# Fewer VectorE instructions in weight preparation and in the aside exponential, and row copies by transfer instead of ScalarE, in a two-layer attention and gated-MLP kernel

## The chip, the cores and the metric

The kernel runs on one core of a Trainium2 chip. The metric is the device time of one execution in microseconds (us); lower is better. The engines are named as the profile names them: PE (TensorE), PEld (its weight loads), DVE (VectorE), ACT (ScalarE), POOL (GpSimd, called Pool below) and SP (SyncE, which here only issues transfers).

## The reference

Two identical layers on x of 2048 tokens by 448 features, in float32. The same weights serve both layers.

```python
def _A_ref(x, wqkv, wo):                       # 16 heads of 28
    qkv = (x @ wqkv).reshape(B, S, 3, H, Dh).transpose(2, 0, 3, 1, 4)
    q, k, v = qkv[0], qkv[1], qkv[2]
    p = softmax(einsum("bhqd,bhkd->bhqk", q, k) * Dh ** -0.5)
    return einsum("bhqk,bhkd->bhqd", p, v).transpose(0, 2, 1, 3).reshape(B, S, D) @ wo
def _B_ref(x, w_gate, w_up, w_down):           # F = 1792
    return (sigmoid(x @ w_gate) * (x @ w_up)) @ w_down
x = x + _A_ref(layernorm(x), wqkv, wo)
x = x + _B_ref(layernorm(x), w_gate, w_up, w_down)
# ... the same two lines once more
```

## The kernel before, in words

**Numbers in two parts.** PE multiplies float16 tiles. A float32 operand is held as a high part (its float16 rounding) and a low part (what that left out), and a product is high by high, low by high and high by low.

**Half tiles.** The q/k projection and the gate and up products use Strassen's scheme with sums of quarter blocks. A block of 512 tokens is prepared by `Block.half_steps`: 10 or 11 small steps named after the quarters and differences (`r11, t1, t2, t3, r21, t4, r22, [r12], last_low, last_rows`), which leave the tiles `wide` (four operands) and `short` (three or four); ACT makes the high parts (`high`), DVE the differences and low parts (`subtract`, `low`). Of the 448 features the last 64 half-fill a tile, so the upper 64 partitions of some slots are free; `again` (L486) copies 64 rows of high parts into such a slot with ACT, and `last_rows` (L547, L548) adds and copies 64 more rows. A block is "turned" when its features come by PE transposes (the first block of each gated stage, two in all); the other blocks read them back through memory. Twelve blocks are made in all.

The weights for these products are made once, in layer 0, by `split_sums`: for a pair of weight tiles it forms four sums (`add_up`, L263), 14 high half tiles (L269) and their low parts (L272) in one float16 tile `t` of 27 slots (`N_SUMS`), with Pool copying some 64-partition halves (L290, L291) and DVE adding one pair (L292). The tile is written to memory (`gu_parts`, `qs_parts`, L1409) and loaded where it is used. `of_halves` (L656) multiplies; `LOW_A`, `TAILS` and `SHORT` say which slots it takes.

**Attention.** 16 heads x 16 key tiles x 4 query blocks make 1024 units of 128 keys by 512 queries in a layer. PE computes scores (L1524) for three units at a time, ACT takes their exponential in one instruction (L1539), and PE accumulates the product with the values (L1575) into `acc`. Of the 1024 units, 33 in layer 0 and 48 in layer 1 are "aside": PE writes their scores to another PSUM bank and DVE computes the exponential with a polynomial (`score_aside`, L1549 to L1558). The aside units of head h use bank `1 - h % 2`, which held `acc` of head h-1; so their scores wait until DVE has moved that `acc` out (`finish`, first instruction L1604). The order is written out by hand, one program order for all engines. In layer 0, from key tile 4 of the first head on, the class `Prepare` runs one step of weight preparation every few key tiles (`along`); its instructions go into DVE's queue between the asides and the finishes. `Prepare` makes 17 calls of `split_sums` (14 for gate and up, 3 for q and k).

**After attention.** The output projection, the layernorm and the gated stage follow by blocks of 512 tokens. The gated stage of layer 0 hands over to the projection of layer 1 (near 980 to 1040 us in the trace), where ACT makes the high parts of the last blocks and the values (L1109), and moves PE's results out (L955); PE's next product waits for a PSUM bank that these free.

Of the kernel before, what the change touches and what calls it, by code (L numbers as in the profile page):

```python
# [45 lines left out]
GUARD_LIMIT = 72.0  # L46


POWER_OF_2 = (1.0000001192092896, -0.6931469440460205, 0.24022120237350464,
              -0.05550713464617729, 0.009675540030002594, -0.0013276454992592335)  # L50
ROUND = 12583039.0

N_SUMS = 27
PLACES = 0, 3, 1, 2
DN = D // 2

AFTER_USUAL = ((0, 3), (0, 4), (1, 0), (1, 2))
N_DN = 8
USUAL = 2
LOW_A = 14, 15, 16, 17
TAILS = 1, 24, 25, 26
SHORT = ((10, 12, 20, 22), (11, 13, 21, 23), (8, 9, 18, 19))

# [60 lines left out]
def interleaved_layers(ctx: ExitStack, tc: tile.TileContext, x_in, wqkv, wo, w_gate, w_up,  # L128
# [137 lines left out]
    def split_sums(t, v, by):  # L266

        def high(to, a):
            nc.vector.tensor_scalar(to, a, by, None, op0=ALU.mult)  # L269

        def low(to, hi, a):
            nc.vector.scalar_tensor_tensor(to, a, by[0:hi.shape[0]], hi, op0=ALU.mult,  # L272
                                           op1=ALU.subtract)
# [16 lines left out]
        nc.gpsimd.tensor_copy(t[0:64, 24:27], t[0:64, 3:8:2])  # L290
        nc.gpsimd.tensor_copy(t[64:P, 7], t[64:P, 23])  # L291
        nc.vector.tensor_tensor(t[64:P, 19], t[64:P, 19], t[64:P, 23], op=ALU.add)  # L292
        qrt.put(*sums)

    def powers(c, n, squares):
# [20 lines left out]
    class Block:  # L316
# [128 lines left out]
        def half_steps(self):  # L445
# [21 lines left out]
            def high(to, v):  # L467
                hi = to[:, 0]
                if len(v.shape) == 5:
                    for k in range(2):  # L470
                        nc.scalar.copy(ordered(hi)[:, k], v[:, k])
                else:
                    nc.scalar.copy(hi, v)
# [7 lines left out]
                else:  # L481
                    nc.vector.tensor_tensor(lo, v, hi, op=ALU.subtract)  # L482

            def again(to):

                nc.scalar.copy(to[64:P, 1, 1], to[0:64, 0, 1])  # L486

            def r11():
                self.wide = big.get("xwide", [P, 4, 2, 2, W // 2], F16)
# [10 lines left out]
            def t2():  # L500
                low(self.wide[:, 1], self.t1)
                self.t3 = subtract("t3", cut(2, 2), cut(0, 2))
                high(self.wide[:, 2], self.t2)
                again(self.wide[:, 0])
                qrt.put(self.t1)

            def t3():
                low(self.wide[:, 2], self.t2)
                self.t4 = subtract("t4", cut(2, 0), self.t2)
                high(self.wide[:, 3], self.t3)  # L510
                again(self.wide[:, 1])
                qrt.put(self.t2)

            def r21():
                self.short = big.get("xshort", [P, 4 if self.whole else 3, 2, 2, W // 2], F16)
                low(self.wide[:, 3], self.t3)
                high(self.short[:, 0], cut(2, 0))
                again(self.wide[:, 2])
                qrt.put(self.t3)

            def t4():
                low(self.short[:, 0], cut(2, 0))
                high(self.short[:, 1], self.t4)
                again(self.wide[:, 3])
# [118 lines left out]
    def of_halves(pm, w, blk, k, first):  # L643


        if k < 4:
            x = blk.wide[:, k]
            terms = [(w[:, 2 * k], x[:, 0, 0]), (w[:, 2 * k], x[:, 1, 0]),
                     (w[:, LOW_A[k]], x[:, 0, 0]),
                     (w[:, 2 * k + 1], x[:, 0, 1]), (w[:, TAILS[k]], x[:, 1, 1])]  # L650
        else:
            x = blk.short[:, k - 4]
            terms = [(w[:, SHORT[k - 4][i]], x[:, j, t])
                     for t in range(2) for i, j in ((t, 0), (t, 1), (2 + t, 0))]
        for i, (a, x) in enumerate(terms):
            nc.tensor.matmul(pm, a, x, start=(first and i == 0),  # L656
                             stop=(i == len(terms) - 1), skip_group_check=True)
# [20 lines left out]
    class WeightsQKV:  # L678
# [73 lines left out]

        def load_rest(self):
            self.alone = [t[:, 28:32] for t in self.held[1:]]
            self.v_tail = self.held[0][:, N_SUMS:31].rearrange("p k n -> p (k n)")[:, 0:D]
# [740 lines left out]
    def attend(layer, values, heads, last_values, gate, wq):  # L1496
# [44 lines left out]
        def score_aside(u):  # L1541
# [4 lines left out]
            t = qrt.get("whole", [P, W])  # L1546
            p = qrt.get("power", [P, W])
            c = POWER_OF_2
            nc.vector.tensor_scalar(y, ps, base2[:, 0:1], -126.0, op0=ALU.mult, op1=ALU.max)  # L1549
            nc.vector.tensor_scalar(t, y, ROUND, None, op0=ALU.add)  # L1550
            nc.vector.scalar_tensor_tensor(y, t, ROUND, y, op0=ALU.subtract, op1=ALU.subtract)
            nc.vector.tensor_scalar(p, y, c[5], c[4], op0=ALU.mult, op1=ALU.add)
# [4 lines left out]
            nc.vector.tensor_scalar(whole, whole, 23, None, op0=ALU.logical_shift_left)  # L1557
# [698 lines left out]
```

## Time and profile before

| | before |
|---|---|
| median of 3 runs | 1896.03 us (1894.89 to 1896.67) |
| profiled execution | 1894.65 us, of which the span of the trace is 1892.9 |
| granted clock of PE in it | 0.999 |
| busy share of the span | PE 99%, DVE 80%, ACT 76%, POOL 14% |

The 1.75 us between span and device time lie outside the trace. PE's ends are modelled and its instructions pipelined, so its 99% does not say that it never waits; the waits are listed by themselves. Attention of layer 0 lies at about 120 to 578 us, attention of layer 1 at about 1060 to 1510 us, the gated stages at about 600 to 1010 and 1530 to 1893 us. In the rows below, "x" gives the count, `[2.50 <-DVE oturned_q L1604]` says that the engine stood idle for 2.50 us before this row and what ended that, and a line with "q" behind the engine is its queue's own work (issuing a transfer).

### The profile page before, as it was taken

How to read it: one execution, taken by the hardware profiler on the slowest of the kernel's cores; microseconds unless marked ns; L12 is line 12 of the kernel's file. 1: busy time of each engine (PE TensorE's matmuls, PEld its weight loads, DVE VectorE, ACT ScalarE, POOL GpSimd, SP SyncE). 2: the span in 40 equal slices, each digit the busy share in tenths (PEclk: the TensorE clock that was granted, in tenths of full speed). 3: DMA queues.
4: the chain of work that ended last, by engine and by line, in shares of the span. 5: the costliest groups of instructions: out<-in, count | busy, mean ns of one | idle time of the engine just before them, and what ended most of it. 6: DMA issues, size and time to landing. Idle time of an engine off the chain costs nothing. (4 is left out here: it accounts for less than half of the span.)

```text
span 1892.9 us, 57291 instructions
## 1 busy us (share of the span) xinstructions
PE 1869.3 (99%) x24485; PEld 1396.0 (74%) x24485; DVE 1512.9 (80%) x3081; ACT 1431.1 (76%) x1913; POOL 267.5 (14%) x526
## 2 busy tenths in 40 slices
PE   9999999999999999999999999999999999999999
PEld 4456566655655889999977567677787568999999
DVE  7748999998997888788877577777787788887764
ACT  5569999999994655565567799999999846555541
POOL 3001123333311111212110000000000020121110
PEclk9999999999999999999999999999999999999999
DMA  7674454343423755656653421221120247566653
GB/s 255 186 212 127 130 160 125 121 137 117 132 82 127 265 212 210 249 222 240 230 171 105 116 52 28 50 52 32 47 52 12 73 129 276 193 246 242 236 219 142
DMA packets 116709, 284.47 MB, mean 150 GB/s; under 512 B 14878, under 2 KB 72718, under 8 KB 116320
## 3 DMA queue, kind: packets, MB, share of 16 engines
q0 software_dynamic: 32496, 171.09, 24.9%
q1 hardware_dynamic: 82800, 108.27, 20.0%
q8 instruction: 194, 3.18, 0.7%
q10 hardware_dynamic: 1152, 1.38, 0.3%
q14 instruction: 67, 0.55, 0.1%
HBM read 218.10 MB, written 54.19 MB: 144 GB/s over the span
## 5 line engine op out<-in xcount | busy, mean ns | idle before, releaser
L1539 ACT ACTIVATE prob_s<-sc 128x1536 f32<-128x1536 f32 (+1 forms) x657 | 889.9, 1469 | 17.5 <-PE sc L1524 14.6
L1575 PE MATMUL acc<-prob_s,val_s 128*32 128x256 f32 (+3 forms) x7708 | 584.2, 384 | 0.0
L1524 PE MATMUL sc<-qp_s 114*32 114x512 f16 x7868 | 568.4, 380 | 0.0
L656 PEld LDWEIGHTS <-gu_s 128*128 128x128 f16 x4256 | 415.7, 98 | 47.7 <-issue 2.6
L1524 PEld LDWEIGHTS <-qp_s 114*32 114x32 f16 x8192 | 301.9, 96 | 189.1 <-issue 82.4
L1575 PEld LDWEIGHTS acc<-prob_s,val_s 128*32 128x32 f32 x7708 | 303.1, 110 | 111.8 <-issue 10.8
L1884 PE MATMUL dnp<-dn_s,hparts_s 128*128 128x224 f16 x2184 | 246.0, 259 | 0.0
L1884 PEld LDWEIGHTS <-hparts_s 128*128 128x128 f16 x2184 | 210.2, 98 | 5.2
L656 PE MATMUL chain<-xwide_s,gu_s 128*128 128x256 f16 x1680 | 210.8, 273 | 0.3
L1555 DVE SCALAR_TENSOR_TENSOR power_q<-power_q,expo_q 128x512 f32<-128x512 f32 x243 | 168.2, 692 | 8.3
L656 PE MATMUL side<-xshort_s,gu_s 128*128 128x256 f16 x1344 | 165.0, 273 | 1.1 <-DVE one_q L1973 1.1
L1957 ACT COPY one_q<-chain 128x256 f32<-128x256 f32 x224 | 81.7, 372 | 97.4 <-PE chain L656 96.0
L1973 DVE TENSOR_TENSOR one_q<-side,one_q 128x512 f32<-128x512 f32 x112 | 74.9, 690 | 71.7 <-PE side L656 71.4
L1765 POOL DMA_DIRECT2D gu_s<-gu_parts x104 | 56.1, 540 | 428.5 <-PE side L656 419.7
L1837 ACT CAST hparts_s<-hsums_q 128x256 f16<-128x256 f32 (+1 forms) x152 | 71.5, 485 | 44.4 <-DVE hsums_q L1849 30.9
L1575 PE MATMUL acc<-power_q,val_s 128*32 128x256 f32 (+3 forms) x300 | 94.3, 396 | 0.0
L1984 ACT ACTIVATE one_q<-one_q 128x512 f32<-128x512 f32 x56 | 35.3, 631 | 72.8 <-DVE one_q L1973 72.7
L1604 DVE STREAM_TRANSPOSE oturned_q<-acc 128x512 f32<-128x512 f32 x32 | 22.9, 717 | 81.1 <-PE acc L1575 80.8
L656 PE MATMUL chain<-xshort_s,gu_s 128*128 128x256 f16 x672 | 82.5, 273 | 0.0
L656 PE MATMUL side<-xwide_s,gu_s 128*128 128x256 f16 x560 | 79.4, 273 | 0.0
L1549 DVE TENSOR_SCALAR expo_q<-aside,base 128x512 f32<-128x512 f32 x81 | 60.6, 748 | 20.7 <-PE aside L1524 20.4
L1841 DVE TENSOR_TENSOR hparts_s<-hsums_q,hparts_s 128x256 f16<-128x256 f32 (+1 forms) x152 | 72.5, 516 | 4.7 <-ACT hparts_s L1837 4.7
(268 smaller groups left out, 2470.4 us busy)
## 6 DMA issues: line engine op xcount, KB each, us to landing
gu_s<-gu_parts POOLq DMA_DIRECT2D x104, 864.0 KB, 6.1
dn_s<-dn_parts POOLq DMA_DIRECT2D x42, 784.0 KB, 7.4
qp_s<-qk_scr SPq DMA_DIRECT2D x96, 224.0 KB
gu_parts<-pack_s POOLq DMA_DIRECT2D x14, 864.0 KB, 5.4
xt_scr<-xs_s SPq DMA_DIRECT2D x48, 224.0 KB
qk_scr<-qkhl_q SPq DMA_DIRECT2D x28, 256.0 KB
qp_s<-qk_scr SPq DMA_DIRECT2D x64, 112.0 KB
qk_scr<-qkhl_q SPq DMA_DIRECT2D x56, 128.0 KB
```

Source lines behind the costliest of these rows:

```text
L656: nc.tensor.matmul(pm, a, x, start=(first and i == 0), stop=(i == len(terms) - 1), skip_group_check=True)
L1524: nc.tensor.matmul(ps[32 * j:32 * j + 32, :], hd.k[:, keys], hd.q[:, qb * W:(qb + 1) * W], start=True, stop=True, tile_position=(0, 32 * j))
L1539: nc.scalar.activation(prob[:, 0:n, :], ps[:, 0:n, :], AF.Exp, scale=exp_scale)
L1549: nc.vector.tensor_scalar(y, ps, base2[:, 0:1], -126.0, op0=ALU.mult, op1=ALU.max)
L1555: nc.vector.scalar_tensor_tensor(p, p, c[k], y, op0=ALU.add, op1=ALU.mult)
L1575: nc.tensor.matmul(acc[qb * VC:(qb + 1) * VC, s], v[:, kc % TB, h, :], probs[c * NB + qb][:, s], start=(kc == 0 and a == 0), stop=(kc == N ...
L1765: queue.dma_start(self.gu[-1][m], gu_parts[p, m])
L1837: nc.scalar.copy(to[:, :, 0], a)
L1841: nc.vector.tensor_tensor(to[:, :, 1], a, to[:, :, 0], op=ALU.subtract)
L1884: nc.tensor.matmul(pm, a[:, x, t], w[:, p, y], start=(begin and n == 0 and (j == 0 or alone)), stop=(n == 2), skip_group_check=True)
L1957: nc.scalar.copy(to, pm)
L1973: nc.vector.tensor_tensor(one[m], side[m], one[m], op=ALU.add)
```

## The change

Three edits.

- **Aside exponential.** The polynomial of degree 5 becomes a monic one of degree 5, so that its first step (a scaling by two constants, L1552) falls away: 10 DVE instructions become 9. Two of the others change form: rounding is one TENSOR_SCALAR with two constants, the fraction a TENSOR_TENSOR; and the shift of an integer (L1557) becomes an add and a multiply in float whose result is written as int32.
- **`split_sums`.** The low parts stand in the same order as the high parts, so four DVE instructions make them instead of eight, and the add remains. Pool copies 64x128 once and 64x4x128 twice, all behind the low parts; before it copied 64x384 behind the high parts and 64x128 behind one of the low parts. A tile has 28 slots instead of 27, and the transfers that write and load it grow with it.
- **`half_steps`.** In blocks that are not turned, the ACT copies of `again` become one transfer on SP's queue for the four `wide` operands, issued in step `r22` (and one for `short[:, 3]`, where there is one), and the copy of `last_rows` becomes a transfer too. In turned blocks the four ACT copies move together to step `r22`. The add of `last_rows` moves from DVE to Pool, behind the copy.

```diff
-POWER_OF_2 = (1.0000001192092896, ..., -0.0013276454992592335)
-ROUND = 12583039.0
-N_SUMS = 27
+POWER_OF_2 = (753.2155151367188, 522.0890502929688, 180.93832397460938,
+              41.808834075927734, 7.287768840789795)
+LEAD = 117.35950469970703
+ROUND = 12582912.0
+N_SUMS = 28
...
-        for to, hi, a in ((t[:, 14], t[:, 0], v[:, 0, 0]),
-                          (t[:, 15:17], t[:, 2:6:2], s12[:, 0:4:2]),
-                          (t[:, 17:19], t[:, 6:10:2], s34[:, 0:4:2]),
-                          (t[:, 19], t[:, 9], s34[:, 3]),
-                          (t[:, 20:24].rearrange("p (k z) n -> p k z n", k=2),
+        for to, hi, a in ((t[:, 14:16], t[:, 0:2], v[:, 0:2, 0]), (t[:, 16:20], t[:, 2:6], s12),
+                          (t[:, 20:24], t[:, 6:10], s34),
+                          (t[:, 24:28].rearrange("p (k z) n -> p k z n", k=2),
                            t[:, 10:14].rearrange("p (k z) n -> p k z n", k=2), v[:, 2:4])):
             low(to, hi, a)
-        low(t[64:P, 24:26], t[0:64, 3:6:2], s12[0:64, 1:4:2])
-        low(t[64:P, 26], t[0:64, 7], s34[0:64, 1])
-        low(t[64:P, 1], t[0:64, 1], v[0:64, 1, 0])
-        nc.gpsimd.tensor_copy(t[0:64, 24:27], t[0:64, 3:8:2])
-        nc.gpsimd.tensor_copy(t[64:P, 7], t[64:P, 23])
-        nc.vector.tensor_tensor(t[64:P, 19], t[64:P, 19], t[64:P, 23], op=ALU.add)
+        nc.gpsimd.tensor_copy(t[64:P, 7], t[64:P, 27])
+        nc.vector.tensor_tensor(t[64:P, 23], t[64:P, 23], t[64:P, 27], op=ALU.add)
+        nc.gpsimd.tensor_copy(t[64:P, 15:22:2], t[0:64, 15:22:2])
+        nc.gpsimd.tensor_copy(t[0:64, 15:22:2], t[0:64, 1:8:2])
...
-            def again(to):
-                nc.scalar.copy(to[64:P, 1, 1], to[0:64, 0, 1])
+            def again(*tiles):
+                if self.turned:
+                    for to in tiles:
+                        nc.scalar.copy(to[64:P, 1, 1], to[0:64, 0, 1])
+                else:
+                    to = tiles[0].rearrange("p (a h) t n -> p a h t n", a=1) if len(
+                        tiles) == 1 else self.wide
+                    nc.sync.dma_start(to[64:P, :, 1, 1], to[0:64, :, 0, 1])
...
             def r22():
                 low(self.short[:, 1], self.t4)
                 high(self.short[:, 2], cut(2, 2))
+                again(*[self.wide[:, k] for k in range(4)])
...
-                nc.vector.tensor_tensor(rows, rows, lo, op=ALU.add)
-                nc.scalar.copy(self.wide[64:P, 1, 0, 1], lo)
+                if self.turned:
+                    nc.scalar.copy(self.wide[64:P, 1, 0, 1], lo)
+                else:
+                    nc.sync.dma_start(self.wide[64:P, 1, 0, 1], lo)
+                nc.gpsimd.tensor_tensor(rows, rows, lo, op=ALU.add)
...
-            nc.vector.tensor_scalar(y, ps, base2[:, 0:1], -126.0, op0=ALU.mult, op1=ALU.max)
-            nc.vector.tensor_scalar(t, y, ROUND, None, op0=ALU.add)
-            nc.vector.scalar_tensor_tensor(y, t, ROUND, y, op0=ALU.subtract, op1=ALU.subtract)
-            nc.vector.tensor_scalar(p, y, c[5], c[4], op0=ALU.mult, op1=ALU.add)
-            nc.vector.tensor_tensor(p, p, y, op=ALU.mult)
+            nc.vector.tensor_scalar(y, ps, base2[:, 0:1], -116.0, op0=ALU.mult, op1=ALU.max)
+            nc.vector.tensor_scalar(t, y, ROUND, ROUND, op0=ALU.add, op1=ALU.subtract)
+            nc.vector.tensor_tensor(y, y, t, op=ALU.subtract)
+            nc.vector.scalar_tensor_tensor(p, y, c[4], y, op0=ALU.add, op1=ALU.mult)
             for k in (3, 2, 1):
                 nc.vector.scalar_tensor_tensor(p, p, c[k], y, op0=ALU.add, op1=ALU.mult)
-            whole = t.bitcast(I32)
-            nc.vector.tensor_scalar(whole, whole, 23, None, op0=ALU.logical_shift_left)
+            nc.vector.tensor_scalar(t.bitcast(I32), t, LEAD, 2.0 ** 23, op0=ALU.add,
+                                    op1=ALU.mult)
             nc.vector.scalar_tensor_tensor(p, p, c[0], t, op0=ALU.add, op1=ALU.mult)
```

Left out are the calls of `again` that the steps `t2`, `t3`, `r21` and `t4` lose, the renumbered `LOW_A`, `TAILS` and `SHORT`, and a slice for the values' tail that moves by one slot. The order of PE's instructions does not change. Three places show what does. The order lists give line, operation, output and inputs with their buffer numbers, and the shape.

DVE in attention of layer 0, at the last gate/up call of `split_sums`, which runs up to the finish of head 13. `pack_s` is the tile `t`, `raws_s` the loaded weights, `sums_q` the four sums. Before:

```order
L269 TENSOR_SCALAR pack_s_12373<-raws_s_6174,up 128x512
L272 SCALAR_TENSOR_TENSOR pack_s_12373<-raws_s_6174,up,pack_s_12373 128x128
L272 SCALAR_TENSOR_TENSOR pack_s_12373<-sums_q_12374,up,pack_s_12373 128x256
L272 SCALAR_TENSOR_TENSOR pack_s_12373<-sums_q_12375,up,pack_s_12373 128x256
L272 SCALAR_TENSOR_TENSOR pack_s_12373<-sums_q_12375,up,pack_s_12373 128x128
L272 SCALAR_TENSOR_TENSOR pack_s_12373<-raws_s_6174,up,pack_s_12373 128x512
L272 SCALAR_TENSOR_TENSOR pack_s_12373<-sums_q_12374,up,pack_s_12373 64x256
L272 SCALAR_TENSOR_TENSOR pack_s_12373<-sums_q_12375,up,pack_s_12373 64x128
L272 SCALAR_TENSOR_TENSOR pack_s_12373<-raws_s_6174,up,pack_s_12373 64x128
L292 TENSOR_TENSOR pack_s_12373<-pack_s_12373 64x128
L1604 STREAM_TRANSPOSE oturned_q_12526<-acc_11996 128x512
```

After:

```order
L270 TENSOR_SCALAR pack_s_12303<-raws_s_6169,up 128x512
L273 SCALAR_TENSOR_TENSOR pack_s_12303<-raws_s_6169,up,pack_s_12303 128x256
L273 SCALAR_TENSOR_TENSOR pack_s_12303<-sums_q_12304,up,pack_s_12303 128x512
L273 SCALAR_TENSOR_TENSOR pack_s_12303<-sums_q_12305,up,pack_s_12303 128x512
L273 SCALAR_TENSOR_TENSOR pack_s_12303<-raws_s_6169,up,pack_s_12303 128x512
L287 TENSOR_TENSOR pack_s_12303<-pack_s_12303 64x128
L1607 STREAM_TRANSPOSE oturned_q_12453<-acc_11931 128x512
```

Eight instructions of low parts have become four, three of them over 512 elements a partition; the add and the finish keep their places.

Pool at the same call. The transfer is the tile's write, the memset clears the free half of the next loaded weights. Before:

```order
L1389 MEMSET raws_s_6174 64x256
L290 COPY pack_s_12373<-pack_s_12373 64x384
L291 COPY pack_s_12373<-pack_s_12373 64x128
L1409 DMA gu_parts<-pack_s_12373 128x3456
L1385 DMA raws_s_6174<-in_A_wqkv_dram 128x128
```

After:

```order
L1393 MEMSET raws_s_6169 64x256
L286 COPY pack_s_12303<-pack_s_12303 64x128
L288 COPY pack_s_12303<-pack_s_12303 64x4x128
L289 COPY pack_s_12303<-pack_s_12303 64x4x128
L1413 DMA gu_parts<-pack_s_12303 128x3584
L1389 DMA raws_s_6169<-in_A_wqkv_dram 128x128
```

There are three copies where there were two, over 1152 elements a partition instead of 512, still ahead of the write, which is 3.7% larger.

ACT in the projection of layer 1, the first of its later blocks (`xwide_s` and `xshort_s` are `wide` and `short`, `val_s` the values, `vp` and `chain` PSUM banks). Before:

```order
L473 CAST xwide_s_19032<-t_q_19190 128x512
L486 COPY xwide_s_19032<-xwide_s_19032 64x256
L1109 ACTIVATE val_s_18963<-vp_19278 128x16x28
L471 CAST xshort_s_19334<-xraw_s_18745 128x256 x2
L486 COPY xwide_s_19032<-xwide_s_19032 64x256
L1109 ACTIVATE val_s_18963<-vp_19300 128x16x28
L473 CAST xshort_s_19334<-t_q_19294 128x512
L486 COPY xwide_s_19032<-xwide_s_19032 64x256
L1109 ACTIVATE val_s_18963<-vp_19340 128x16x28
L955 COPY one_q_19364<-chain_19362 128x256
```

After:

```order
L470 CAST xwide_s_18933<-t_q_19091 128x512
L1113 ACTIVATE val_s_18864<-vp_19178 128x16x28
L468 CAST xshort_s_19233<-xraw_s_18649 128x256 x2
L1113 ACTIVATE val_s_18864<-vp_19199 128x16x28
L470 CAST xshort_s_19233<-t_q_19194 128x512
L1113 ACTIVATE val_s_18864<-vp_19238 128x16x28
L959 COPY one_q_19261<-chain_19259 128x256
```

The three copies are gone from ACT's queue. What takes their place is on SP's queue; in the last block of the same projection it stands after the change like this (`qk_scr` takes the projection's results):

```order
L930 DMA qk_scr<-qkhl_q_19753 256x1x256 x2
L489 DMA xshort_s_19594<-xshort_s_19594 64x256
L550 DMA xwide_s_19545<-xshort_s_19594 64x256
L930 DMA qk_scr<-qkhl_q_19810 256x1x256 x2
L930 DMA qk_scr<-qkhl_q_19815 256x1x256 x2
```

The two transfers of the step `last_rows` stand between writes of results, in SP's one queue.

More of the change, by code (lines that the diff above doesn't have):

```diff
@@ L46 @@
 GUARD_LIMIT = 72.0
-POWER_OF_2 = (1.0000001192092896, -0.6931469440460205, 0.24022120237350464,
-              -0.05550713464617729, 0.009675540030002594, -0.0013276454992592335)
-ROUND = 12583039.0
-N_SUMS = 27
+POWER_OF_2 = (753.2155151367188, 522.0890502929688, 180.93832397460938,
[3 more added lines that the diff above has]
+N_SUMS = 28
 PLACES = 0, 3, 1, 2
@@ L63 @@
 USUAL = 2
-LOW_A = 14, 15, 16, 17
-TAILS = 1, 24, 25, 26
-SHORT = ((10, 12, 20, 22), (11, 13, 21, 23), (8, 9, 18, 19))
+LOW_A = 14, 16, 18, 20
+TAILS = 15, 17, 19, 21
+SHORT = ((10, 12, 24, 26), (11, 13, 25, 27), (8, 9, 22, 23))
 ASIDE = {1: ((6, 15, 1),), 2: ((4, 10, 3), (9, 15, 1)), 3: ((4, 9, 3), (8, 13, 1), (12, 15, 2))}
@@ L503, in t2 @@
                 high(self.wide[:, 2], self.t2)
-                again(self.wide[:, 0])
                 qrt.put(self.t1)
@@ L510, in t3 @@
                 high(self.wide[:, 3], self.t3)
-                again(self.wide[:, 1])
                 qrt.put(self.t2)
@@ L517, in r21 @@
                 high(self.short[:, 0], cut(2, 0))
-                again(self.wide[:, 2])
                 qrt.put(self.t3)
@@ L523, in t4 @@
                 high(self.short[:, 1], self.t4)
-                again(self.wide[:, 3])
             def r22():
@@ L649, in of_halves @@
                      (w[:, LOW_A[k]], x[:, 0, 0]),
-                     (w[:, 2 * k + 1], x[:, 0, 1]), (w[:, TAILS[k]], x[:, 1, 1])]
+                     (w[:, 2 * k + 1 if k else TAILS[0]], x[:, 0, 1]),
+                     (w[:, TAILS[k]], x[:, 1, 1])]
         else:
@@ L754, in load_rest @@
             self.alone = [t[:, 28:32] for t in self.held[1:]]
-            self.v_tail = self.held[0][:, N_SUMS:31].rearrange("p k n -> p (k n)")[:, 0:D]
+            self.v_tail = self.held[0][:, N_SUMS:32].rearrange("p k n -> p (k n)")[:, 0:D]
             c = slice(ALONE * P, (ALONE + 1) * P)
```

## The prediction

> **What bounds the kernel now.** I read the page's head first, then the windows by stage, then the waits of ACT, PE and DVE, then the timeline at each wait of PE.
>
> ```profile
> span 1892.9 us, 57291 instructions
> PE 1869.3 (99%) x24485; PEld 1396.0 (74%) x24485; DVE 1512.9 (80%) x3081; ACT 1431.1 (76%) x1913; POOL 267.5 (14%) x526
> ```
>
> PE's 99% leaves some 20 us of gaps in all, so a change off PE can give no more than a part of that. Where the gaps are, the windows tell (columns: length, then busy time of PE, PEld, DVE, ACT, POOL).
>
> ```profile
> 200.00:257.25 57.25, 57.25 (x1056) 34.94 (x1048) 52.15 (x101) 57.25 (x44) 8.93 (x14) 1.00 0.42 113
> 257.25:448.50 191.25, 184.68 (x3364) 115.51 (x3360) 184.10 (x379) 184.40 (x137) 66.36 (x117) 1.00 0.47 139
> 464.70:576.70 112.00, 108.93 (x1956) 64.52 (x1952) 107.99 (x218) 107.34 (x81) 26.99 (x50) 0.98 0.38 120
> 1120.00:1500.00 380.00, 380.00 (x6952) 281.81 (x6948) 298.21 (x496) 380.00 (x279) 0.00 (x0) 1.00 0.19 46
> ...
> ACT prob_s L1539 <- PE sc L1524: 11.3, 9, 3.0
> ```
>
> In attention ACT's exponential sets the pace: it is busy for all of 200 to 257 us and 1120 to 1500 us. DVE has room in layer 1, so a shorter aside gives nothing there, 48 of the 81. In layer 0, from 257 us on, ACT loses 191.25 - 184.40 = 6.85 and 112.00 - 107.34 = 4.66, together 11.5 us; the last row (ACT's waits in 257 to 577 us) says that 11.3 of it is nine waits for PE's scores. Why PE is late (waits of PE, then the worst places, then all waits of DVE in 240 to 580 us):
>
> ```profile
> PE aside L1524 <- DVE oturned_q L1604: 8.6, 6, 2.6
> ...
> PE side L656 <- DVE one_q L1973: 1.1, 2, 0.6
> ...
> 438.75 0.40 PE L1524 MATMUL aside<-qp_s 114*32 114x512 f16 x4 [2.50 <-DVE oturned_q L1604]
> 524.81 0.40 PE L1524 MATMUL aside<-qp_s 114*32 114x512 f16 x4 [2.57 <-DVE oturned_q L1604]
> ...
> DVE oturned_q L1604 <- PE acc L1575: 4.6, 2, 3.3
> DVE expo_q L1549 <- PE aside L1524: 1.7, 2, 1.1
> ```
>
> PE's aside scores wait for DVE to clear the bank, and the scores behind them come late to ACT. DVE is late because its queue is full: in all that time it waits four times, and in between it runs without a pause and its delay adds up. So here, and here alone, DVE time is kernel time.
>
> **Exponential, 33 asides of layer 0.** Durations of the lines that change (minimum, median and maximum in ns):
>
> ```profile
> L1549 DVE TENSOR_SCALAR expo_q<-aside,base x81: 740/747/753, 125.9 to 1498.9; 128x512 f32<-128x512 f32 x81
> L1551 DVE SCALAR_TENSOR_TENSOR expo_q<-whole_q,expo_q x81: 691/693/736, 127.1 to 1500.2; 128x512 f32<-128x512 f32 x81
> L1552 DVE TENSOR_SCALAR power_q<-expo_q x81: 426/427/556, 127.9 to 1500.9; 128x512 f32<-128x512 f32 x81
> L1557 DVE TENSOR_SCALAR whole_q<-whole_q x81: 416/419/424, 131.1 to 1504.1; 128x512 int32<-128x512 int32 x81
> ```
>
> L1552 goes: 0.43, with the gap behind it 0.46 us. L1551 and L1553 become each other's form at the same 0.69. Float in and int32 out is not in the trace: 0.42 if it runs like L1557, 0.69 if it falls to the pace of the two-input forms. I take 0.42, since both TENSOR_SCALARs on SBUF run at it whatever their type. Relief per aside 0.46, at worst 0.19.
>
> **`split_sums`, 16 of its 17 calls in the full stretch.** One call (DVE by form, 500 to 530 us, then Pool's copies, then the time line of one call):
>
> ```profile
> L272 DVE SCALAR_TENSOR_TENSOR pack_s<-sums_q,up,pack_s 128x256 f16<-128x256 f32 x4 | 1.7, 472 | 0.0
> L272 DVE SCALAR_TENSOR_TENSOR pack_s<-raws_s,up,pack_s 128x512 f16<-128x512 f32 x2 | 1.5, 738 | 0.0
> L272 DVE SCALAR_TENSOR_TENSOR pack_s<-raws_s,up,pack_s 128x128 f16<-128x128 f32 x2 | 1.2, 592 | 0.0
> L272 DVE SCALAR_TENSOR_TENSOR pack_s<-sums_q,up,pack_s 128x128 f16<-128x128 f32 x2 | 0.7, 340 | 0.0
> ...
> L290 POOL COPY pack_s<-pack_s x17: 497/690/694, 260.0 to 550.5; 64x384 f16<-64x384 f16 x17
> L291 POOL COPY pack_s<-pack_s x17: 290/294/298, 262.5 to 553.2; 64x128 f16<-64x128 f16 x17
> ...
> 506.93 0.69 POOL L290 COPY pack_s<-pack_s 64x384 f16<-64x384 f16 x1 [7.31 <-DVE pack_s L269]
> ...
> 507.18 0.59 DVE L272 SCALAR_TENSOR_TENSOR pack_s<-raws_s,up,pack_s 128x128 f16<-128x128 f32 x1
> 510.67 0.22 DVE L292 TENSOR_TENSOR pack_s<-pack_s 64x128 f16<-64x128 f16 x1
> 510.92 0.75 DVE L1549 TENSOR_SCALAR expo_q<-aside,base 128x512 f32<-128x512 f32 x1
> ```
>
> From the first low to the next job DVE spends 510.92 - 507.18 = 3.74 us. After: 0.40 + 0.66 + 0.66 + 0.77 for the lows (their pitch: 0.472 and 0.738 less the overlap seen between rows, plus the gap) and 0.25 for the add, 2.74. That frees 1.00 us, if Pool's copies cost DVE nothing. They may not: the same low of 128x128 takes 0.59 beside L290 and 0.34 without it, and L290 itself takes 0.69 beside DVE's work and 0.50 at its shortest. Pool now copies 0.29 + 2 x 0.69 x 512/384 (0.92) = 2.1 us, and all of it lies behind the lows, beside the add, an aside or a finish. Lower end of the relief: all 2.1 us block DVE, 1.0 - 2.1 = -1.1. Upper end: 1.0. I take 0.5: the row nearest to it lost 0.25 us beside 0.69 us of copy, 0.36 for each us, which would be 0.75 over 2.1 us; but L1549 and L1604 read PSUM, follow at once, and L1549's 740 to 753 over 81 executions shows no loss beside anything.
>
> [...]
>
> Relief against loss, with the counts of asides (first two rows, L1549) and calls (last two, L292) up to each stretch's last stall:
>
> ```profile
> 245.00:438.75 193.75, 9.71 (x13) 1.00 0.44 130
> 464.70:555.30 90.60, 4.49 (x6) 0.98 0.36 109
> ...
> 245.00:438.75 193.75, 2.22 (x10) 1.00 0.44 130
> 464.70:555.30 90.60, 1.33 (x6) 0.98 0.36 109
> ```
>
> First stretch: 13 x 0.46 + 10 x 0.5 = 11.0 us against 6.85 lost. Second: 6 x 0.46 + 6 x 0.5 = 5.8 against 4.66. Both are covered. Some stays, since within a stretch an early stall has less relief ahead of it than a late one, and each us that ACT wins back leaves DVE a us less for the same work. DVE's rows taken one by one with these reliefs leave about 1 us, near 360 and 379 us; I leave 1.3 of the 11.3. Attention of layer 0: **-10.0 us**. What is late next is ACT itself, which no edit shortens there.
>
> Pool's queue has its copies 1.1 us longer per call, and the write and the next loads of weights behind them. A call comes every 13 to 15 us and the loads are issued one call ahead, so I price that, and the 3.7% more bytes, at nothing; with a lead under 2 us it would not be.
>
> **ACT's copies in the projection of layer 1.**
>
> ```profile
> 987.82 1.25 PE L656 MATMUL chain<-xwide_s,wsums_s 128*128 128x256 f16 x10 [2.06 <-ACT val_s L1109]
> 991.17 1.03 PE L656 MATMUL chain<-xwide_s,wsums_s 128*128 128x256 f16 x8 [1.06 <-ACT one_q L955]
> 1016.75 1.25 PE L656 MATMUL chain<-xwide_s,wsums_s 128*128 128x256 f16 x10 [1.35 <-ACT one_q L955]
> ...
> L486 ACT COPY xwide_s<-xwide_s x48: 402/403/405, 607.4 to 1756.9; 64x256 f16<-64x256 f16 x48
> ```
>
> PE waits here for ACT to free PSUM banks, and ACT runs through its queue with copies in it. Each group of waits has three copies ahead of its last row: 3 x 0.40 = 1.2 us, twice, so -2.4, at most the 4.5 us of these rows, at least nothing if DVE's parts are late instead. Elsewhere ACT's copies and the DVE add of `last_rows` are beside PE's work and give nothing, but for the two turned blocks: there DVE's queue waits for ACT's high parts, which come up to 3 x 0.40 us sooner, and loses the add, so the two waits on L1973 (0.6 at most, 1.1 in sum) should end: **-1.1**, at least nothing.
>
> **The transfers.** They cost where a product needs the rows before they land. The tight place is the last block before attention of layer 1:
>
> ```profile
> 1027.75 8.46 SPq L926 DMA_DIRECT2D qk_scr<-qkhl_q  x8
> ...
> 1031.11 0.71 PE L656 MATMUL side<-xwide_s,wsums_s 128*128 128x256 f16 x5
> ...
> 989.84 1.25 SPq L403 DMA_DIRECT2D xt_scr<-xs_s  x1
> 994.40 0.35 SPq L413 DMA_DIRECT2D xraw_s<-xt_scr  x1
> ```
>
> A write issues in 8.46/8 = 1.06 us, so the two copies behind the first are issued by about 1030.0. The nearest landing is that of the last two rows: issued by 991.09, read at 994.40, 3.3 us and larger; the other end is nothing. The rows are needed at 1031.4 (the fourth product of that `side`), so PE waits 0 to 1.9 us; I take **+0.4**, for a small transfer lands sooner than a 224 KB one. The other blocks have 9 us and more between issue and need. [...] Projection in sum: -2.4 + 0.4 = **-2.0**.
>
> **Sum.** -10.0 - 1.1 - 2.0 = -13.1. The profiled execution took 1894.65 us (span 1892.9 and 1.75 around it), so 1881.5; the median of the runs, 1896.03, stands 1.4 above it: **1882.9 us**.
>
> **Rivals.** About 0.2%, 3.8 us, is what a measurement of this kernel tells from no change.
>
> [...]
>
> [...]
>
> *Slower.* Pool's copies stop DVE for their whole length: -1.1 per call, 19 x 0.46 - 16 x 1.1 = -8.9 us of relief, so the stalls grow by 8.9, less 3.1: +5.8, **1901.8 us**. It is slower than before from 0.74 us lost per call on balance (8.7 + 3.1 over 16), that is from 1.74 us of DVE blocked in each. Against it: L272 at 507.18 was not held for the whole of L290's remaining 0.44 us, only 0.25.
>
> **How the numbers follow.** Forecast 0.67, with its own range 1880.5 to 1886 (1.0 to 0.2 of relief per call, 0 to 1.9 us of landing). Copies take it back 0.19, between 1886 and 1892. Nothing to be seen 0.09. Slower 0.05. So faster 0.86, same 0.09, slower 0.05. The range goes from 1879, where the 11.3, 4.5 and 1.1 us are all gained and no landing costs (16.9 below the median), to 1891, which leaves out some 0.18 above.
>
> **What the next profile would show.** Right: the asides' waits on `oturned_q` fall from 8.6 to about 1 us, ACT is 100% busy from 270 to 576 us, and attention of layer 1 keeps its length. The lows have 0.66 us at 128x512 of sums, the int32 write 0.42, the waits on L1109 and L955 near 987 and 1016 us halve. Wrong: L1550, L1551 or L1606 behind a call well over 0.43 and 0.69 us; Pool copies far over 0.9; a wait of PE on a transfer into `wide` at 1031 us or in a gated block.

## The result and the profile after

The changed kernel took 1880.40 us in the median (1878.03 to 1880.80, 4 runs) against 1895.46 for the kernel before: a ratio of 0.9917, 95% interval 0.9900 to 0.9935. That is 15.1 us faster; forecast were 13.1 us and 1882.9 us. The head of its page:

```profile
span 1878.5 us, 57183 instructions
PE 1864.6 (99%) x24485; PEld 1352.7 (72%) x24485; DVE 1464.1 (78%) x2920; ACT 1405.9 (75%) x1859; POOL 288.0 (15%) x555
```

PE's order did not change, so the same instruction can be looked up in both traces, and the difference of its two start times says how much has been gained up to there. Five such pairs follow, from the timelines of before and of after: the first residual add behind attention of layer 0, a result of the first gated block, the last residual add of layer 0, the last ACT move of the values for layer 1, and the first residual add behind attention of layer 1.

```profile
589.63 0.68 DVE L1708 SCALAR_TENSOR_TENSOR x<-op,back,x 128x448 f32<-128x448 f32 x1 [7.62 <-PE op L1704]
626.85 0.69 DVE L1973 TENSOR_TENSOR one_q<-side,one_q 128x512 f32<-128x512 f32 x1 [0.75 <-PE side L656]
943.81 0.64 DVE L1902 SCALAR_TENSOR_TENSOR x<-dnp,back,x 128x448 f32<-128x448 f32 x1
1015.90 0.54 ACT L1109 ACTIVATE val_s<-vp 128x448 f32<-128x448 f32 x1
1519.13 0.68 DVE L1708 SCALAR_TENSOR_TENSOR x<-op,back,x 128x448 f32<-128x448 f32 x1 [7.61 <-PE op L1704]
```

```profile
576.39 0.68 DVE L1711 SCALAR_TENSOR_TENSOR x<-op,back,x 128x448 f32<-128x448 f32 x1 [7.62 <-PE op L1707]
612.89 0.69 DVE L1976 TENSOR_TENSOR one_q<-side,one_q 128x512 f32<-128x512 f32 x1 [0.75 <-PE side L660]
932.68 0.68 DVE L1905 SCALAR_TENSOR_TENSOR x<-dnp,back,x 128x448 f32<-128x448 f32 x1 [1.41 <-PE dnp L1887]
1001.48 0.53 ACT L1113 ACTIVATE val_s<-vp 128x448 f32<-128x448 f32 x1
1504.69 0.68 DVE L1711 SCALAR_TENSOR_TENSOR x<-op,back,x 128x448 f32<-128x448 f32 x1 [7.66 <-PE op L1707]
```

| Up to | before | after | gained so far | in this stretch |
|---|---|---|---|---|
| end of attention, layer 0 | 589.63 | 576.39 | 13.24 | 13.24 |
| first gated block | 626.85 | 612.89 | 13.96 | 0.72 |
| end of layer 0 | 943.81 | 932.68 | 11.13 | -2.83 |
| projection of layer 1 | 1015.90 | 1001.48 | 14.42 | 3.29 |
| end of attention, layer 1 | 1519.13 | 1504.69 | 14.44 | 0.02 |
| end of the span | 1892.9 | 1878.5 | 14.4 | 0.0 |

So nearly all of it lies in attention of layer 0, as forecast. The projection gave more than forecast, and the gated stage of layer 0 took 2.8 us back, which was not forecast at all. Attention of layer 0 in the windows, to its last exponential (columns as before), and DVE's waits in it (240 to 570 us):

```profile
257.25:576.70 319.45, 309.80 (x5596) 189.69 (x5592) 304.65 (x624) 307.94 (x229) 97.05 (x173) 0.99 0.43 129
...
257.25:563.50 306.25, 306.25 (x5597) 178.75 (x5591) 281.56 (x531) 306.24 (x229) 108.48 (x190) 1.00 0.46 138
...
DVE oturned_q L1607 <- PE acc L1578: 12.0, 8, 4.8
DVE expo_q L1553 <- PE aside L1528: 6.7, 4, 2.2
```

The first row is before, the second after: the same 229 exponentials, and ACT is now busy for all of the 306.25 us. DVE waits 18.7 us where it waited 6.3; it is no longer the late one. PE's waits after:

```profile
PE dnp L1887 <- DMA dn_s<-dn_parts: 1.8, 1, 1.8
PE chain L660 <- ACT val_s L1113: 1.8, 1, 1.8
...
PE chain L660 <- DMA gu_s<-gu_parts: 1.0, 1, 1.0
PE chain L660 <- ACT two_q L1960: 0.6, 2, 0.3
```

The waits of 8.6 us on the bank (`oturned_q`) are gone from the list. Two waits on transfers and two on `two_q` are new: 3.4 us. The three of them that stand in the gated stage of layer 0 (1.8, 1.0 and 0.3 us) cover the 2.8 us that it took back.

### The profile page after: what moved, and what is told of

Read it like the earlier page. It is cut to its first block, busy times and chain, and to the rows that moved or that the text cites. A ratio compares the mean times of both kernels' runs of the same rounds, so it can differ in the third digit from the quotient of the medians.

```text
span 1878.5 us, 57183 instructions
## 1 busy us (share of the span) xinstructions
PE 1864.6 (99%) x24485; PEld 1352.7 (72%) x24485; DVE 1464.1 (78%) x2920; ACT 1405.9 (75%) x1859; POOL 288.0 (15%) x555
## 3 DMA queue, kind: packets, MB, share of 16 engines
q10 hardware_dynamic: 1152, 1.38, 0.3%
## 5 line engine op out<-in xcount | busy, mean ns | idle before, releaser
L1578 PE MATMUL acc<-prob_s,val_s 128*32 128x256 f32 (+3 forms) x7708 | 573.5, 383 | 0.0
L1528 PE MATMUL sc<-qp_s 114*32 114x512 f16 x7868 | 556.5, 379 | 0.0
L1528 PEld LDWEIGHTS <-qp_s 114*32 114x32 f16 x8192 | 279.6, 96 | 196.8 <-issue 83.9
L1578 PEld LDWEIGHTS acc<-prob_s,val_s 128*32 128x32 f32 x7708 | 280.3, 110 | 137.1 <-issue 11.7
L1553 DVE TENSOR_SCALAR expo_q<-aside,base 128x512 f32<-128x512 f32 x81 | 60.6, 748 | 40.4 <-PE aside L1528 40.0
```

The source lines that it names most:

```text
L1528: nc.tensor.matmul(ps[32 * j:32 * j + 32, :], hd.k[:, keys], hd.q[:, qb * W:(qb + 1) * W], start=True, stop=True, tile_position=(0, 32 * j))
L1553: nc.vector.tensor_scalar(y, ps, base2[:, 0:1], -116.0, op0=ALU.mult, op1=ALU.max)
L1578: nc.tensor.matmul(acc[qb * VC:(qb + 1) * VC, s], v[:, kc % TB, h, :], probs[c * NB + qb][:, s], start=(kc == 0 and a == 0), stop=(kc == N ...
```

## Experiments

**Each edit alone, and the changed kernel without one of its parts.** The four kernels ran on one chip, with the kernel before at 1896.25 us.

*e1: the kernel before, with the new exponential.*

```diff
...
-            nc.vector.tensor_scalar(p, y, c[5], c[4], op0=ALU.mult, op1=ALU.add)
-            nc.vector.tensor_tensor(p, p, y, op=ALU.mult)
...
+            nc.vector.scalar_tensor_tensor(p, y, c[4], y, op0=ALU.add, op1=ALU.mult)
...
```

> The kernel before with the new exponential alone. Theory (DVE's queue): in attention of layer 0 each us that DVE is freed of ahead of a stall shortens it by one, until ACT sets the pace. 19 asides in the full stretches x 0.46 = 8.7 us at most, 6 where the relief comes too late for the early stalls; attention of layer 0 shortens by 6 to 9 us, layer 1's by nothing, and 3 to 6 us of waits on the bank stay: 1886.5 to 1889.5 us. Rival (the gain lies in the low parts and Pool's copies beside them): under 2 us, 1893.5 or more.

*e2: the kernel before, with the new `split_sums` and its 28 slots.*

```diff
...
-        low(t[64:P, 24:26], t[0:64, 3:6:2], s12[0:64, 1:4:2])
-        low(t[64:P, 26], t[0:64, 7], s34[0:64, 1])
-        low(t[64:P, 1], t[0:64, 1], v[0:64, 1, 0])
...
+        nc.gpsimd.tensor_copy(t[64:P, 15:22:2], t[0:64, 15:22:2])
+        nc.gpsimd.tensor_copy(t[0:64, 15:22:2], t[0:64, 1:8:2])
...
```

> The kernel before with the new split_sums alone, with its 28 slots. Theory (DVE's queue): 16 calls x 0.70 us (1.0 less the 0.27 that the changed kernel's rows lose to Pool's copies) = 11.2 us at most of the 13.2 that attention of layer 0 lost, 9.5 where it comes too late: 1884 to 1886 us before any loss elsewhere. If the larger weight transfers cause the wait of 1.0 us on gu_s in the first gated block, it is here too; if it is the earlier start of that block (the other edit), it is not. Rival (edits add up without overlap): the gains of this and of the exponential alone sum to the 13.2 us of both; by the theory they sum to more, 15 to 20.

*e3: the kernel before, with the new `half_steps`.*

```diff
-                nc.scalar.copy(to[64:P, 1, 1], to[0:64, 0, 1])
...
+                    nc.sync.dma_start(to[64:P, :, 1, 1], to[0:64, :, 0, 1])
...
-                nc.vector.tensor_tensor(rows, rows, lo, op=ALU.add)
...
+                nc.gpsimd.tensor_tensor(rows, rows, lo, op=ALU.add)
```

> The kernel before with the change of half_steps alone (copies by transfers, the add on Pool). Theory: attention of both layers as before; the two turned blocks give 1.1 us each, the projection of layer 1 some 3, and the wait of 1.8 us on dn_s near the end of the first gated stage is here, because the add on Pool stands ahead of the issue of those loads: in sum -3 to -4, 1891.5 to 1892.5 us. Rival for that wait (the weight transfers of 28 slots crowd the DMA engines): no wait on dn_s here, -5 us, 1890.5.

*e4: the changed kernel, with that add back on DVE.*

```diff
-                nc.gpsimd.tensor_tensor(rows, rows, lo, op=ALU.add)
+                nc.vector.tensor_tensor(rows, rows, lo, op=ALU.add)
```

> The changed kernel with the add of last_rows back on DVE, all else as it is. Theory (Pool's add waits for ACT's and DVE's parts and holds up the loads issued behind it): the loads of dn_s near 921 us are issued some 3 us sooner and the wait of 1.8 us at 928 goes; 1.8 us below the changed kernel's 1880.4, 1878.6 us, or up to 1 us less of that where the add of 0.29 us is in DVE's way in the turned blocks. Rival (the transfers themselves are late): the wait stays, 1880.4 us or more.

| | median us | ratio to before, 95% | attention of layer 0 against before |
|---|---|---|---|
| e1, exponential | 1889.19 | 0.9958 (0.9944 to 0.9971) | -6.9 |
| e2, split_sums | 1884.65 | 0.9942 (0.9929 to 0.9956) | -9.8 |
| e3, half_steps | 1892.49 | 0.9987 (0.9977 to 0.9996) | +1.5 |
| e4, all but the add | 1878.14 | 0.9904 (0.9889 to 0.9919) | -13.2 |

(The last column is read off the pair at 589.63 us of before. Nine of e3's eleven runs took 1891.2 to 1893.6 us, two 1899.3 and 1899.6.) PE's waits on the bank in e1, in e2 and in e3, one row each, and in e3 the wait on `dn_s`:

```profile
PE aside L1525 <- DVE oturned_q L1604: 4.6, 5, 1.5
...
PE aside L1521 <- DVE oturned_q L1601: 2.4, 3, 1.5
...
PE aside L1530 <- DVE oturned_q L1610: 10.3, 6, 2.6
...
PE dnp L1890 <- DMA dn_s<-dn_parts: 0.6, 1, 0.6
```

Each of the two DVE edits removes a part of the waits by itself, 6.9 and 9.8 us; together they would be 16.7 us, and both at once give 13.2, because then ACT sets the pace (busy for 306.24 of 306.25 us above). That is the queue theory; the rivals (the gain lies in the low parts alone; the edits add up) fall. The half-tile edit does not touch attention; its 1.5 us there come from the granted clock in that execution (last section). In the other stretches of the table above e3 gives 0.72 us up to the first gated block and 3.29 in the projection, as the changed kernel does. It has the wait on `dn_s` with 27 slots, so the wait does not need the larger transfers. But it is 0.6 us there, where 1.8 were expected, and 0.8 to 1.8 in the six profiles that have the 28 slots as well; whether the larger transfers lengthen it is not shown. In e2, which has the 28 slots, no wait on `gu_s` or `dn_s` stands in PE's list.

Why the add on Pool costs: Pool's rows before the down products in the changed kernel with PE's wait there, and then Pool's rows in e10, which is e4 once more.

```profile
921.06 0.72 POOL L551 TENSOR_TENSOR xshort_s<-xshort_s 64x256 f16<-64x256 f16 x1 [14.63 <-ACT hparts_s L1840]
921.74 1.61 POOL L1781 DMA_DIRECT2D dn_s<-dn_parts  x3
...
928.46 1.79 PE L1887 MATMUL dnp<-dn_s,hparts_s 128*128 128x224 f16 x17 [1.82 <-DMA dn_s<-dn_parts]
...
917.03 1.18 POOL L1781 DMA_DIRECT2D dn_s<-dn_parts  x2 [11.79 <-PE side L660]
920.92 0.53 POOL L1781 DMA_DIRECT2D dn_s<-dn_parts  x1 [2.71 <-DVE xshort_s L476]
```

In Pool's rows the loads of `dn_s` stand behind the add, which Pool starts at 921.06 us after 14.63 us of idle time, and they follow it at 921.74; in e10 two of the three are issued from 917.03 us on. PE stands for 1.8 us at 928. (Without that wait the products would stand at 926.6; in e10 they stand at 925.6, so the loads are some 3.7 us later against the products.)

**e7: the changed kernel once more.**

> The changed kernel once more, unaltered, for its profile. If the wait of 1.0 us on gu_s at 622 us comes from the program (its order and bytes) it is there again; if it is a transfer that landed late in that one execution, it is not, and the wait on dn_s at 928 us, which comes from the add on Pool's queue, is there either way: 1878 to 1881 us.

It took 1879.00 us. The wait on `gu_s` at 622 us is not in it, the wait on `dn_s` is (1.5 us). So the first was mostly one execution's late landing (0.3 us of it are in e8 and 0.2 in e10, none in e9): in the first profile the four loads of `gu_s` in 605 to 625 us landed 9.0 us after their issue in the median, in this one 7.2.

**e5: Pool's two large copies left out.**

```diff
-        nc.gpsimd.tensor_copy(t[64:P, 15:22:2], t[0:64, 15:22:2])
-        nc.gpsimd.tensor_copy(t[0:64, 15:22:2], t[0:64, 1:8:2])
```

> The changed kernel without Pool's two 64x4x128 copies in split_sums (leaves those rows of the tiles unmade). [...] Rival (the copies still set the pace there): attention of layer 0 shorter by 1 us or more.

In the changed kernel, what stands behind one call (DVE, then Pool), and then the lines of the first two-input instructions of an aside and of a finish in e5:

```profile
496.30 0.48 DVE L273 SCALAR_TENSOR_TENSOR pack_s<-raws_s,up,pack_s 128x256 f16<-128x256 f32 x1
...
498.81 0.22 DVE L287 TENSOR_TENSOR pack_s<-pack_s 64x128 f16<-64x128 f16 x1
499.06 0.75 DVE L1553 TENSOR_SCALAR expo_q<-aside,base 128x512 f32<-128x512 f32 x1
499.85 0.43 DVE L1554 TENSOR_SCALAR whole_q<-expo_q 128x512 f32<-128x512 f32 x1
500.31 0.98 DVE L1555 TENSOR_TENSOR expo_q<-expo_q,whole_q 128x512 f32<-128x512 f32 x1
...
499.22 0.61 POOL L288 COPY pack_s<-pack_s 64x512 f16<-64x512 f16 x1
499.89 0.85 POOL L289 COPY pack_s<-pack_s 64x512 f16<-64x512 f16 x1
...
L1553 DVE TENSOR_TENSOR expo_q<-expo_q,whole_q x81: 691/693/695, 127.3 to 1483.6; 128x512 f32<-128x512 f32 x81
...
L1607 DVE TENSOR_TENSOR oturned_q<-oturned_q,rec x32: 691/693/697, 151.9 to 1492.4; 128x512 f32<-128x512 f32 x32
```

The instruction that reads PSUM (L1553) runs beside the first large copy and keeps its 0.75 us (0.741 to 0.753 in all 81). The one with two SBUF inputs (L1555) meets the second and takes 0.98 instead of 0.69; in a finish (L1609) the longest takes 0.95. Without the copies none of either line is longer than 0.70. Attention of layer 0 is as long as in the changed kernel within 0.1 us (+0.11 at the first residual add), and e5 took 1878.17 us in its one run, so the rival falls: DVE has these 0.29 us to spare.

**e6 and e8: more copies.** In e6 the pair of copies stands in a loop of three; in e8 each copy is issued three times in a row. The edit of e8:

```diff
-        nc.gpsimd.tensor_copy(t[64:P, 15:22:2], t[0:64, 15:22:2])
-        nc.gpsimd.tensor_copy(t[0:64, 15:22:2], t[0:64, 1:8:2])
+        for _ in range(3):
+            nc.gpsimd.tensor_copy(t[64:P, 15:22:2], t[0:64, 15:22:2])
+        for _ in range(3):
+            nc.gpsimd.tensor_copy(t[0:64, 15:22:2], t[0:64, 1:8:2])
```

> The changed kernel with each of Pool's two 64x4x128 copies done three times, four more copies of 0.61 us a call. [...] Sharing theory (a loss of 0.36 for each us of copy, as beside the copies of the kernel before): 0.9 us more per call, relief -0.2, 8 to 11 us longer, 1888 to 1891. Rival (DVE's instructions on PSUM cover them): within 3 us of the changed kernel.

Repeated in turn, the first copy writes high parts where low parts belong. With such weights the kernel's guard for large scores takes its long way ahead of layer 1 (850 us of row maxima, at 1057 to 1907 us), so e6's 2748.5 us say nothing of the copies. Only attention of layer 0, ahead of that, can be read: 9.7 us longer than in the changed kernel. e8 repeats the test cleanly.

> The changed kernel with each of Pool's two 64x4x128 copies issued three times in a row, so that what they write stays the same: four more copies a call. By the rows of the run before, DVE loses 0.29 us (0.98 instead of 0.69) for every copy that runs beside a two-input instruction and nothing beside the others: up to 1.4 us behind a call that an aside follows, 0.75 behind one that a finish follows, relief per call -0.4 to 0.2. Attention of layer 0 is 8 to 11 us longer than in the changed kernel, everything else as there: 1888 to 1891 us, so that most of the change's gain is gone. Rival (the loss lies in what Pool's queue holds up, the write and the loads behind the copies): DVE waits on the loaded weights (L264) and its rows keep 0.69.

e8 took 1889.37 us (ratio 0.9964, 0.9951 to 0.9977); attention of layer 0 is 11.2 us longer than in the changed kernel, a little over the 8 to 11 expected. Its rows behind one call, and PE's waits:

```profile
510.86 0.98 DVE L1557 TENSOR_TENSOR expo_q<-expo_q,whole_q 128x512 f32<-128x512 f32 x1
511.87 0.98 DVE L1558 SCALAR_TENSOR_TENSOR power_q<-expo_q 128x512 f32<-128x512 f32 x1
512.89 2.00 DVE L1560 SCALAR_TENSOR_TENSOR power_q<-power_q,expo_q 128x512 f32<-128x512 f32 x2
...
509.77 2.54 POOL L289 COPY pack_s<-pack_s 64x512 f16<-64x512 f16 x3
512.37 2.98 POOL L291 COPY pack_s<-pack_s 64x512 f16<-64x512 f16 x3
...
PE aside L1530 <- DVE oturned_q L1609: 4.4, 4, 2.0
PE aside L1530 <- DVE expo_q L1555: 2.9, 1, 2.9
```

The four two-input instructions in these rows take 0.98 to 1.0 us each, 4 x 0.29 = 1.2 us lost behind a call with an aside. Summed over attention of layer 0, DVE's instructions beside a copy are 18.8 us longer than the shortest of their kind, against 3.6 in the changed kernel; attention grew by less than the difference, since DVE had time to spare there. The waits on the bank are back and more than half of the gain is gone (against before in its own runs 6.8 us are left, where the unaltered changed kernel, e9 below, has 16.3 on the same chip). DVE's only wait on loaded weights here is one of 1.4 us in all of attention, so what Pool's queue holds up is at most a small part of the 11.2. e6's 9.7 us lie in the 8 to 11 that a loss of 0.36 us for each us of copy gave, e8's 11.2 a little above them. The rows show what it is made of: 0.29 us for each two-input instruction of 0.69 that meets a copy, and a copy that grows as well (2.98 us for three instead of 1.8), so that the two together take 1.0 us, where 0.61 + 0.69 = 1.3 would be the one behind the other; those that read PSUM lose nothing (L1555 0.745 us and L1609 0.717 in the mean of 250 to 560 us). Instructions with one input in SBUF are not all spared: in e8 the cast behind each of eight finishes loses 0.22 us.

**The better version, beside the changed kernel.**

> The changed kernel, unaltered, beside the next one on the same chip: 1878 to 1881 us, with the wait of 1.3 to 1.8 us on dn_s.

> The changed kernel with the add of last_rows back on DVE, again, beside the unaltered one: without the wait on dn_s and the two of 0.3 us on L1960, 1.5 to 2.5 us below it, 1876.5 to 1879. If the difference between the two in the earlier runs was scatter between chips, they are within 0.5 us.

On one chip e9 took 1879.82 us (1878.60 to 1880.70) and e10 1877.29 (1876.97 to 1877.32): 2.5 us less, with no run of the one in the range of the other. Against before, e10 stands at 0.9901 (0.9885 to 0.9916). The wait on `dn_s` is 1.8 us in e9's profile and absent in e10's; the two waits on `two_q`, 0.6 us together, go too. The traces say why: the add on Pool has two SBUF inputs and stands beside an instruction of DVE that has two as well. Pool and DVE in the changed kernel, the same DVE line over the whole of e10, and the first wait of the two:

```profile
643.82 0.67 POOL L551 TENSOR_TENSOR xshort_s<-xshort_s 64x256 f16<-64x256 f16 x1
644.00 0.78 DVE L1990 SCALAR_TENSOR_TENSOR two_q<-two_q,two_q 128x256 f32<-128x256 f32 x1
...
L1990 DVE SCALAR_TENSOR_TENSOR two_q<-two_q,two_q x56: 424/426/427, 608.3 to 1842.9; 128x256 f32<-128x256 f32 x56
...
646.51 1.25 PE L660 MATMUL chain<-xwide_s,gu_s 128*128 128x256 f16 x10 [0.31 <-ACT two_q L1960]
```

That instruction loses 0.35 us, and the sums that ACT splits next come late by as much. Exactly two of its 56 are long (0.76 to 0.78 us) in each of the six other profiles with the add on Pool, and none in the five with the add on DVE.

## Why the prediction was right, step by step

The forecast of 1882.9 us missed the measured 1880.40 by 2.5, and the gain of 13.1 us the measured 15.1 by 2.0. The measured time lies within 1879 to 1891, and 0.1 us under the 1880.5 to 1886 that the forecast itself was given. That it came so close is in part luck: attention gave 3.2 and the projection 1.3 us more than forecast, and the gated stage of layer 0 took back 2.8 that the sum had at nothing.

- **Where the time is.** DVE's lateness in attention of layer 0, nothing in layer 1: shown by e1, e2 and the table (13.24 and 0.02 us).
- **Attention of layer 0: -10.0 forecast, -13.24 measured.** The mechanism held, two sizes did not. First, the term was capped at the 11.3 us of ACT's idle time. The 229 exponentials take 306.24 us in one piece and 307.94 with nine pauses: neighbours overlap by some 0.14 us (a mean of 1.475 us each before, a pace of 306.24/229 = 1.337 after), and each pause loses that too, 1.2 us in nine; what the rest of the 1.70 is was not taken apart. 11.51 + 1.70 = 13.21 us was there to win. Second, 1.3 us were left as waits, and none stayed. A call gave 0.7 us instead of 0.5 (next point), which may be why; no run tests that by itself.
- **Relief per call: 0.5 forecast.** The lows and the add take 499.06 - 496.30 = 2.76 us in the call above, against 2.74 forecast, and Pool's copies 0.34 + 0.61 + 0.61 = 1.6 us by themselves, not 2.1. They cost DVE at most 0.29 us behind every call but one, and 0.70 behind the one at 340 us, where the next call's sums (L264, two SBUF inputs) follow at once. Of the 3.74 us before, 3.74 - 2.76 = 0.98 are freed, and 0.98 - 0.29 = 0.7 are left, between the 0.5 taken and the upper end of 1.0. The reason given, that PSUM-reading instructions come first, is what the rows show (L1553 keeps its 0.75 us beside a copy). In the call above the one that lost had two SBUF inputs, 0.29 us beside a copy of 0.61. No run shows that the change's copies cost DVE as much as the chances of 0.19 (they take the relief back) and 0.09 (nothing to be seen) stand for; the rows show the 0.29 and 0.70 us above. The lead of 2 us, under which the loads behind the copies were to have a price, is the author's estimate; no run varies it.
- **Relief per aside: 0.46.** The row with float input and int32 output takes 0.42 us, as taken:

```profile
L1559 DVE TENSOR_SCALAR whole_q<-whole_q x81: 418/420/431, 130.7 to 1489.2; 128x512 int32<-128x512 f32 x81
```

- **Turned blocks: -1.1.** Each of the two first gated blocks gave 0.72 (626.85 to 612.89 us in layer 0, 1556.34 to 1541.18 in layer 1), 1.4 in sum, and both waits on L1973 left PE's list. Of the second block's 0.72 nothing is left at the end of the span: 0.3 us go in a wait on `two_q`, 0.4 behind the last residual add.
- **Projection of layer 1: -2.0 forecast, -3.3 measured.** PE's waits there fell from 2.06, 1.06 and 1.35 us, 4.47 in sum, to these two, 2.21, close to the 2.4 taken for the copies. Smaller waits that the prediction had left out went with them (two of 0.34 and one of 0.23 us): in the lists of waits of this stretch the sum falls from 5.7 to 2.7 us, which is nearly all of the 3.3. The gain comes from the copies and not from the add, since with the add back on DVE it is still there (3.7 us in e4, 3.2 in e10):

```profile
976.20 1.25 PE L660 MATMUL chain<-xwide_s,wsums_s 128*128 128x256 f16 x10 [1.76 <-ACT val_s L1113]
...
978.45 1.25 PE L660 MATMUL chain<-xwide_s,wsums_s 128*128 128x256 f16 x10 [0.45 <-ACT one_q L959]
```

  The +0.4 for landing in the last block did not come. That a small transfer lands sooner than one of 224 KB, from which it was taken, no run shows for SP's queue, whose landings are not listed; on Pool's queue in the kernel before, the loads of `raws_s` landed 4.4 to 5.2 us after their issue at 32 to 128 KB and 5.7 us at 224 KB, in the medians. The last row transfer was issued from 1015.21 to 1015.80, and PE's products on these rows, from 1016.68 on, stand in no list of waits:

```profile
1015.21 0.59 SPq L550 DMA_DIRECT2D xwide_s<-xshort_s  x1
...
1016.68 0.80 PE L660 MATMUL side<-xwide_s,wsums_s 128*128 128x256 f16 x5
```

- **What failed: "elsewhere ... the DVE add of `last_rows` ... give nothing".** The add was costed on the queue that it left, not on the one that it joined. On Pool it holds up the loads of `dn_s`: 1.8 us in the changed kernel (e9), none with the add on DVE (e10). Beside DVE's instructions it costs the two waits on `two_q`, 0.6 us, as well. Larger terms went the other way, so the sum hid it.

## What to carry to other kernels

Where one engine's queue runs without pauses and is waited for, count its time ahead of each wait: relief is worth what it says up to the point where the next engine sets the pace, and two reliefs of the same wait do not add (here 6.9 and 9.8 us by themselves, 13.2 together). A moved instruction must be priced in the queue that it joins, above all if it waits there and transfers are issued behind it (here 1.8 us of PE's time in e9, none in e10). When a copy goes to Pool, look at which DVE instructions stand beside it: those reading PSUM paid nothing here (0.75 us with and without a copy), those of 0.69 us with two SBUF inputs up to 0.29 us per copy of 0.61.

## What the runs showed of the hardware that was not expected

Some waits of PE cost 1.7 us more than their length here, which is also a part of ACT's idle time above. Two waits of the kernel before, of 2.50 us up to 438.75 and of 2.57 us up to 524.81, each in a stretch of 3.41 us that holds it or a part of it, and the 3.41 us behind that stretch (PE's busy time stands behind the length, the granted clock is the third column from the right):

```profile
436.93:440.34 3.41, 1.59 (x32) 0.97 (x35) 3.24 (x8) 0.97 (x1) 1.84 (x4) 1.00 0.25 100
440.34:443.75 3.41, 3.41 (x70) 1.88 (x66) 3.24 (x7) 3.38 (x3) 2.86 (x5) 1.00 0.87 287
522.26:525.67 3.41, 0.86 (x16) 0.51 (x19) 3.25 (x8) 1.66 (x2) 1.40 (x4) 1.00 0.00 0
525.67:529.08 3.41, 3.41 (x41) 1.89 (x37) 3.24 (x7) 1.45 (x1) 3.41 (x6) 0.50 0.95 325
```

Behind the second wait the clock is 0.50 and 41 products run; behind the first it stays at 1.00 and 70 run. In e3, whose attention is the same program, it is the other way round: of two waits of 2.61 us the one up to 438.63 is followed by a clock of 0.50, the one up to 526.36 is not.

In these traces the two differ in how the wait lies on a grid of time. In each of the twelve the granted clock changes only at instants that are whole multiples of 3.413 us apart (within 0.004 us): in the kernel before at 6.85, 525.67 and 529.09 us, 152 and 1 of them apart; the two drops of e8, at 360.79 and 439.29 us, are 23 of them apart. The stretches above are two windows of this grid with their next. In the first PE was idle for 3.41 - 1.59 = 1.82 us, since an instant of the grid cuts the wait in two, in the second for 2.55. Over all twelve traces, from 20 us to the end (in e6 up to 1040 us), six windows were followed by a drop, which then lasted one window; in these PE was idle for 2.02 to 2.69 us. In all other windows it was idle for 1.85 us or less. Five of the six lie in attention of layer 0 (before, e3, e6 and two in e8), one in the projection of e1, behind a wait of 2.25 us. This is read from the traces, by PE's modelled ends; no run was made to test it. The grid lies elsewhere in each execution: the wait near 438 us has its window from 436.93 in the kernel before and from 435.77 in e3.

One drop cost 1.7 us, half of its window. In e3 PE's products are 0.12 us ahead of the kernel before at 438 us and 1.56 behind at 442; past the drop that only the kernel before has, at 529 us, they are 0.13 ahead again. DVE is not: it frees the bank 1.55 us later in e3 at 526.36 (before, 524.81) and still at 556.85 (555.30), where PE then waits 2.17 us instead of 0.50. In attention of layer 0 DVE waits 3.3 us for scores in e3 and 1.7 in the kernel before. So e3's +1.5 is the drop at 438 us, which DVE, late already, handed on, and what the drop at 525 us took from PE in the kernel before came back as a shorter wait. The runs show the price too: of the 15 runs of the kernel before beside e1 to e4, the two with a mean clock of 1.000 took 1894.3 and 1894.6 us, those with 0.998 or 0.999 1896.1 to 1897.5, those with 0.997 1897.8 and 1898.0.
